# The last unit of a two-layer transformer kernel: full-row matmuls, token tile by token tile

## The chip, the cores and the metric

The kernel runs on one core of one Trainium2 chip. The metric is the device time of one execution in microseconds (us); the time before is the median of three runs. A profile is one further execution, with its own time. Its *span* runs from the first to the last instruction that the profiler recorded.

## What is computed

Two layers, each of attention and a feed-forward part, on x of 2048 tokens by 448 features, in float32:

```python
x = A_x
x = x + _A_ref(_layernorm(x, axis=-1), A_wq, A_wk, A_wv, A_wo)
x = x + _B_ref(_layernorm(x, axis=-1), B_w_gate, B_w_up, B_w_down)
x = x + _A_ref(_layernorm(x, axis=-1), A_wq, A_wk, A_wv, A_wo)
x = x + _B_ref(_layernorm(x, axis=-1), B_w_gate, B_w_up, B_w_down)
...
def _B_ref(x, w_gate, w_up, w_down):
    g = _silu(x @ w_gate)
    u = x @ w_up
    return (g * u) @ w_down
```

The attention (16 heads, one shared key and value head) is not touched by the change. The weights of the feed-forward part are 448 x 1792 (gate, up) and 1792 x 448 (down).

## The kernel before

**Products.** Every float32 operand is kept as a high part and a low part in TensorE's fp32r type. A product takes three passes: high by high, high by low, low by high. In names, `xh`/`xl` are the parts of the normalized x, `wgh`/`wgl` of the gate and up weights, `wdh`/`wdl` of the down weights, and `hh`/`hl` (both inside the tile `h`) of the hidden values g * u.

**Tiling of the feed-forward part.** Tokens come in 4 chunks `c` of 512 (4 token tiles `t` of 128 each), hidden features in 14 slices `fc` of 128, taken two at a time in 7 groups `fs`. For each group the kernel goes over the chunks, and for each chunk over the two slices. One such step is a *unit* (`unit`, L971): gate and up for 512 tokens and 128 hidden features into two PSUM banks `pg[0]` and `pg[1]`; then Silu on ScalarE (L1006), the product with up on VectorE (L1007), `hh` on ScalarE (L1008) and `hl` on VectorE (L1011). The *down* projection of the unit (`down`, L844) adds 4 token tiles of 128 x 448 into four banks `d[0]` to `d[3]`, which collect over the two slices of a group. After the second slice `accumulate` (L873) adds these banks to the residual `xres`: tiles 0, 1 and, in the last group of the last layer, 3 on VectorE (L881), tile 2 by a copy on ScalarE (L884) and an add on GpSimd (L885). In the last group of the last layer each tile is then stored to the output (L888) on SP's queue, except tile 2 of the last chunk, which goes on ScalarE's.

**Half rows.** 448 features are three blocks of 128 and one of 64. Most units split each matmul into two of 64 partitions that run side by side on the two halves of TensorE (`side_by_side`, L327; `by_rows`, L314): 11 pairs, then 10 pairs. Each half must write another bank than its neighbour, and the second set writes the bank that the first set's other half wrote. Between the sets `between` (L336) lets ScalarE copy one column out of each bank (tile `seen`, L339), so that the second set waits until the first is through. A down projection is done likewise: `step` runs 6 pairs (12 half-row matmuls), `between` touches the four banks, and a second `step` runs 6 pairs more. Only the first two units of each layer use full rows for gate and up (`product_T`, L304): 11 matmuls of 128 partitions per bank.

**Order of the work.** A unit does not run its own down projection. It leaves it in `self.pend`, a list of functions, and the next unit takes it: after the first 11 pairs it calls the first down step (L988), then it runs the 10 pairs; after Silu, the multiply and `hh` it calls the second down step, and behind that the adds of the chunk if there are any. What the last unit leaves is run by `flush` (L965): both steps of its down, then `add(0)`, then the other adds. The order of each engine's instructions is that of the program text. After `flush` each engine loads one value (`whole`) and branches past a second copy of the program, which these data never enter.

The *last unit* is layer 1, group 6, chunk 3, slice 13. The down ahead of it is that of slice 12, the one behind it that of slice 13; both write the same four banks, which the order rows below call bank4_17568, bank5_17569, bank6_78 and bank7_79 (tiles 0 to 3). Its gate and up write bank0_17564 and bank1_17565.

Of the kernel before, what the change touches and what calls it, by code (L numbers as in the profile page):

```python
# [15 lines left out]
P = 128  # L16
S = 2048
D = 448
# [5 lines left out]
NC = S // 512  # L24
NG = H // 4
NF = F // P
# [29 lines left out]
def forward(  # L56
# [14 lines left out]
    nc = tc.nc  # L71
# [39 lines left out]
    def bank(cands, hold=False):  # L111

        for _ in cands:
            turn[cands] = (turn.get(cands, -1) + 1) % len(cands)
            b = cands[turn[cands]]
            if b not in live:
                if hold:
                    live.add(b)
                return b, banks[b]
        raise AssertionError("no bank")  # L120

    def halves(name):

        return pers.tile([P, 2, 512], F32R, tag="halves", name=name, bufs=2)
# [151 lines left out]
    def natural(po, squares):  # L276

        if not squares:
            return po
        return po.rearrange("p (g t w) -> p t g w", g=4, w=32)  # L280

    def in_order(a, squares):

        return a.rearrange("p (t g w) -> p t g w", g=4, w=32) if squares else a
# [19 lines left out]
    def product_T(po, a_h, a_l, tiles):  # L304

        xh, xl = tiles[:2]
        seq = []
        for k in range(3):
            seq += [(a_h[k], xh[:, k, :]), (a_h[k], xl[:, k, :]), (a_l[k], xh[:, k, :])]
        seq += [(a_h[3], xh[:, 3, :]), (a_l[3], xh[:, 3, :])]  # L310
        for i, (a, b) in enumerate(seq):
            nc.tensor.matmul(po, a, b, start=(i == 0), stop=(i == len(seq) - 1))  # L312

    def by_rows(upper, n, w, tiles):  # L314

        h, l = w[:2]
        xh, xl, xd = tiles
        rs = slice(64, 128) if upper else slice(0, 64)
        seq = []
        for k in range(3):  # L320
            seq += [(h[rs, k, n, :], xh[rs, k, :]), (h[rs, k, n, :], xl[rs, k, :]), (l[rs, k, n, :], xh[rs, k, :])]
        seq.append((h[rs, 3, n, :], xh[rs, 3, :]))
        if n == upper:
            seq.append((l[rs, 3, n, :], xd[rs, :] if upper else xh[rs, 3, :]))
        return seq

    def side_by_side(lower, upper):  # L327

        assert len(lower) == len(upper)
        for two in zip(lower, upper):  # L330
            for po, (a, b), start, stop in two:
                nc.tensor.matmul(po, a, b, start=start, stop=stop, skip_group_check=True)  # L332
# [3 lines left out]
    def between(*pos):  # L336

        for i, po in enumerate(pos):
            nc.scalar.copy(seen[:, i : i + 1], po[:, 0:1])  # L339
# [495 lines left out]
    groups = [range(f, min(f + FG, NF)) for f in range(0, NF, FG)]  # L835

    class FeedForward:
# [6 lines left out]
        def down(self, fs, fc, d, hh, hl):  # L844


            _, _, dh, dl = self.W[fc]
            self.flip = 1 - self.flip
            one, two = ((0, 1), (2, 3)) if self.flip else ((2, 3), (0, 1))

            def step(ts, first):
                lists = []
                for upper, half in enumerate(ts):
                    rs = slice(64 * upper, 64 * upper + 64)
                    lists.append(
                        [
                            (
                                d[t][:, 0:D],
                                (a[rs, P * t : P * t + P], b[rs, :]),
                                first and fc == fs[0] and z == 0,  # L860
                                not first and fc == fs[-1] and z == 2,
                            )
                            for t in half
                            for z, (a, b) in enumerate(((hh, dh), (hh, dl), (hl, dh)))
                        ]
                    )
                side_by_side(*lists)
                if first:
                    between(*d)

            return [lambda: step((one, two), True), lambda: step((two, one), False)]

        def accumulate(self, gi, c, d):  # L873

            end = gi == len(groups) - 1
            last = end and self.layer == 1

            def add(t):
                r = xres[:, 4 * c + t, :]
                if t < 2 or (t == 3 and last):  # L880
                    nc.vector.tensor_tensor(r, d[t][:, 0:D], r, ALU.add)  # L881
                else:
                    s = self.stage.tile([P, 512], F32, name="stage")[:, 0:D]
                    nc.scalar.copy(s, d[t][:, 0:D])  # L884
                    nc.gpsimd.tensor_tensor(r, s, r, ALU.add)  # L885
                if last:
                    q = nc.scalar if t == 2 and c == NC - 1 else nc.sync
                    q.dma_start(outs[:, 4 * c + t, :], r)  # L888

            def others():  # L890
                for t in (1, 2, 3) if last else (2, 1, 3):
                    add(t)
                live.difference_update(HIGH)
                if end and self.nxt:
                    self.hand_over(c)

            return [lambda: add(0), others]
# [73 lines left out]
        def unit(self, gi, c, n):  # L971
            fs = groups[gi]
            fc = fs[n]
            w = self.W[fc]
            held, pg = zip(*(bank(LOW, True) for _ in range(2)))
            first, self.pend = self.pend, []
            if self.X[c][2] is not None:
                mid = self.mid.pop((gi, c, n), [])
                lists = [by_rows(upper, b, w, self.X[c]) for b in range(2) for upper in range(2)]
                ends = [(i == 0, False) for i in range(11)], [(False, i == 9) for i in range(10)]  # L980
                side_by_side(
                    [(pg[0], o, *e) for o, e in zip(lists[0], ends[0])],
                    [(pg[1], o, *e) for o, e in zip(lists[3], ends[0])],
                )
                between(*pg)
                for f in mid[:1]:
                    f()
                first.pop(0)()  # L988
                for f in mid[1:]:
                    f()  # L990
                side_by_side(
                    [(pg[1], o, *e) for o, e in zip(lists[2], ends[1])],
                    [(pg[0], o, *e) for o, e in zip(lists[1], ends[1])],
                )
            else:
                for b in range(2):
                    product_T(pg[b], *([v[:, k, b, :] for k in range(4)] for v in w[:2]), self.X[c])
                if first:
                    first.pop(0)()
                    self.left.append(first.pop(0))  # L1000
            live.difference_update(held)
            two = halves("h2")
            hh, hl = two[:, 0, :], two[:, 1, :]
            sg = pers.tile([P, 512], F32, name="sg")
            sq = c < NC - 1
            nc.scalar.activation(in_order(sg, sq), natural(pg[0], sq), AF.Silu)  # L1006
            nc.vector.tensor_tensor(in_order(sg, sq), natural(pg[1], sq), in_order(sg, sq), ALU.mult)  # L1007
            nc.scalar.copy(hh, sg)  # L1008
            for f in first[:2]:
                f()  # L1010
            nc.vector.tensor_tensor(hl, sg, hh, ALU.subtract)  # L1011
            for f in first[2:]:
                f()
            for e in list(self.soon):
                e[0] -= 1
                if e[0] < 0:
                    self.soon.remove(e)
                    e[1]()
            if n == 0:
                self.dn[c] = [bank(HIGH, True)[1] for _ in range(4)]  # L1020
            d = self.dn[c]
            self.pend = self.down(fs, fc, d, hh, hl)
            if n == len(fs) - 1:
                self.pend += self.accumulate(gi, c, d)
            if c == NC - 1 and fc + FG + 1 < NF:
                self.pend.append(lambda: self.W.__setitem__(fc + FG + 1, weights(fc + FG + 1)))
# [63 lines left out]
    fs, got = norm_steps(0)  # L1090
# [23 lines left out]
    for c in range(1, NC):  # L1114
        fs, got = norm_steps(c)
# [39 lines left out]
```

## Time and profile before

| | us |
|---|---|
| median of three runs | 1962.71 (1962.13 to 1963.45) |
| the profiled execution | 1962.25 |
| its span | 1960.4 |
| outside the span | 1.85 |
| mean granted TensorE clock | 0.998 of full |
| TensorE busy in the span | 1943.3 |
| start of the last unit, from the span's start | 1941.5 |

In the rows of the timeline the numbers are start and duration in us, then engine, line, operation, what is written from what is read, the partitions and columns, and how many instructions were merged into the row (x2). PE is TensorE's matmuls, PEld its weight loads, SPq and ACTq the queues from which SP and ScalarE issue DMAs. In the chain of waits a row is a piece of the chain that ended last. In a table of stretches the columns are the length, the busy time of PE, PEld, DVE, ACT and POOL, the granted clock, the DMA engines' share and GB/s.

### The profile page before, as it was taken

To read this page: it belongs to the slowest core of one execution; us is meant where nothing else is said; L and a number is where in the kernel's file an instruction comes from. 1 tells how busy PE (TensorE), PEld (TensorE's weight loads), DVE (VectorE), ACT (ScalarE), POOL (GpSimd) and SP (SyncE) were. 2 spreads that over 40 slices of the span, in tenths; PEclk is the share of its full clock that TensorE was granted. 3 is DMA by queue.
4 is the path that set the end of the run, shared out by engine and by line. 5 is a ranking of instruction groups with operands and counts; after the bars stand their busy time and mean duration, and the time that the engine had idled before them with its cause. 6 is when DMAs were issued, how large, how long until landed. Compare 5 with 4: busy or idle time off the path is not lost.

```text
span 1960.4 us, 44004 instructions
## 1 busy us (share of the span) xinstructions
PE 1943.3 (99%) x18469; PEld 1325.5 (68%) x18469; DVE 968.3 (49%) x1638; ACT 1264.1 (64%) x1888; POOL 553.6 (28%) x593
## 2 busy tenths in 40 slices
PE   9999999999999999999999999999999999999998
PEld 7544545445468999999974445454454799988886
DVE  6656575665743223223666565657656433223223
ACT  4899898998943333333349998989989333333332
POOL 4213123132214333333341221121231332323320
PEclk9999999999999999999999999999999999999999
DMA  5111011121130011110251110110211200011102
GB/s 166 55 36 29 21 40 40 29 53 43 26 87 20 17 32 32 32 29 19 67 156 34 37 30 22 50 28 24 67 40 32 71 28 21 17 32 32 32 2 77
DMA packets 100643, 83.61 MB, mean 43 GB/s; under 512 B 25080, under 2 KB 81656, under 8 KB 100440
## 3 DMA queue, kind: packets, MB, share of 16 engines
q1 hardware_dynamic: 98888, 79.55, 14.7%
q8 instruction: 145, 2.38, 0.5%
q10 hardware_dynamic: 1552, 1.20, 0.2%
q14 instruction: 58, 0.48, 0.1%
HBM read 57.38 MB, written 21.50 MB: 40 GB/s over the span
## 4 chain that ended last, share of the span: by engine, by line
PE 87%; ACT 9%; DMA 1%; DVE 1%; issue 1%; POOL 0%; SPq 0%; ACTq 0%; POOLq 0%; DVEq 0%
PE bank L332 40%; PE bank L688 20%; PE bank L633 14%; ACT pt L655 6%; PE three L633 5%; PE bank L312 4%; ACT pair L656 2%; PE three L612 2%; PE bank L612 1%; PE three L621 0%; PE bank L438 0%; DMA kt<-stage 0%; DMA xd<-xh 0%; DMA wr<-in_A_wq_dram 0%; DVE vt L546 0%
## 5 line engine op out<-in xcount | busy, mean ns | idle before, releaser
L655 ACT ACTIVATE pt<-three 128x1536 f32<-128x1536 f32 x512 | 723.0, 1484 | 52.9 <-PE three L633 52.9
L688 PE MATMUL bank<-pt,vsb 128*32 128x512 f32 x3072 | 490.8, 599 | 0.0
L688 PE MATMUL bank<-pair,vsb 128*32 128x512 f32 x1024 | 487.5, 598 | 0.6 <-ACT pair L656 0.6
L633 PE MATMUL bank<-qstack,keys 32*128 32x512 f32 x1536 | 473.1, 425 | 0.0
L332 PE MATMUL bank<-xh,wgh 64*128 64x512 f32 x1728 | 450.7, 389 | 0.0
L633 PE MATMUL three<-qstack,keys 32*128 32x512 f32 x4608 | 428.7, 408 | 0.5 <-ACT stage L539 0.3
L633 PEld LDWEIGHTS bank<-qstack,keys 32*128 32x128 f32 x1536 | 243.5, 183 | 250.0 <-issue 124.9
L654 DVE COPY pair<-bank 128x512 f32<-128x512 f32 x512 | 354.0, 691 | 95.2 <-PE bank L633 57.4
L332 PE MATMUL bank<-xh,wgl 64*128 64x512 f32 x1404 | 371.7, 391 | 0.0
L332 PE MATMUL bank<-xl,wgh 64*128 64x512 f32 x1296 | 338.1, 390 | 0.0
L332 PE MATMUL bank<-wdh,h 64*128 64x448 f32 x1792 | 334.3, 364 | 1.1 <-ACT h L1008 0.8
L1007 DVE TENSOR_TENSOR sg<-bank,sg 128x512 f32<-128x512 f32 x112 | 77.4, 691 | 502.5 <-ACT sg L1006 500.3
L656 ACT ACTIVATE pair<-pair 128x1024 f32<-128x1024 f32 x256 | 281.5, 1100 | 0.0
L332 PEld LDWEIGHTS bank<-xh,wgh 64*128 64x128 f32 x1728 | 266.3, 185 | 16.7 <-issue 1.3
L633 PEld LDWEIGHTS three<-qstack,keys 32*128 32x128 f32 x4608 | 261.5, 183 | 13.9 <-DVE xres L604 1.5
L885 POOL TENSOR_TENSOR xres<-stage,xres 128x448 f32<-128x448 f32 x108 | 127.3, 1197 | 502.5 <-ACT stage L884 502.3
L688 PEld LDWEIGHTS bank<-pt,vsb 128*32 128x32 f32 x3072 | 101.9, 109 | 246.0 <-issue 153.1
L332 PEld LDWEIGHTS bank<-wdh,h 64*128 64x128 f32 x1792 | 247.5, 184 | 14.8 <-issue 2.0
L697 DVE TENSOR_TENSOR o<-bank,o 128x512 f32<-128x512 f32 x224 | 154.9, 691 | 203.8 <-PE bank L688 203.8
L339 ACT COPY seen<-bank 128x1 f32<-128x1 f32 x664 | 81.9, 163 | 254.3 <-PE bank L332 251.2
L332 PEld LDWEIGHTS bank<-xh,wgl 64*128 64x128 f32 x1404 | 219.2, 184 | 13.8
L332 PE MATMUL bank<-wdl,h 64*128 64x448 f32 x896 | 222.2, 367 | 0.0
(145 smaller groups left out, 2095.7 us busy)
## 6 DMA issues: line engine op xcount, KB each, us to landing
o<-rd SPq DMA_DIRECT2D x32, 256.0 KB
qraw<-qd SPq DMA_DIRECT2D x128, 56.0 KB
qd<-stage SPq DMA_DIRECT2D x28, 224.0 KB
wdr<-in_B_w_down_dram SPq DMA_DIRECT2D x28, 224.0 KB
xt<-tb SPq DMA_DIRECT2D x24, 224.0 KB
wr<-in_B_w_gate_dram SPq DMA_DIRECT2D x28, 192.0 KB
wr<-in_B_w_up_dram SPq DMA_DIRECT2D x28, 192.0 KB
xn<-xt SPq DMA_DIRECT2D x6, 768.0 KB
```

The lines of the kernel that those rows point to most:

```text
L312: nc.tensor.matmul(po, a, b, start=(i == 0), stop=(i == len(seq) - 1))
L332: nc.tensor.matmul(po, a, b, start=start, stop=stop, skip_group_check=True)
L339: nc.scalar.copy(seen[:, i : i + 1], po[:, 0:1])
L612: nc.tensor.matmul(po[:, 0:D], a[:, g, P * t : P * t + P], b[:, g, :], start=False, stop=(g == NG - 1 and z == 2), skip_group_check=True,)
L633: nc.tensor.matmul(three[:, j, :] if j < 3 else one, k[js, kp, ks], q[js, part, :], start=(z == 0), stop=(z == 2), tile_position=(32 * j, 0),)
L654: copies.append(nc.vector.tensor_copy(pt1, one))
L655: es.append(nc.scalar.activation(pt, threes[y], AF.Exp, scale=SCALE))
L656: es.append(nc.scalar.activation(pair, pair, AF.Exp, scale=SCALE))
L688: nc.tensor.matmul(to[32 * j : 32 * j + 32, :], vsb[:, n % NT, :], pts[n][j], start=(y == 0), stop=(y == 1), skip_group_check=True,)
L697: f = nc.vector.tensor_tensor(accs[i][:, 0, :], to, accs[i][:, 0, :], ALU.add)
L885: nc.gpsimd.tensor_tensor(r, s, r, ALU.add)
L1007: nc.vector.tensor_tensor(in_order(sg, sq), natural(pg[1], sq), in_order(sg, sq), ALU.mult)
```

## The change

The last unit, and the downs of the last group of the last chunk, take another form:

- Gate and up of the last unit run in full rows with `product_T`: 11 matmuls for gate, then 11 for up, with no `between`.
- The down projections of slices 12 and 13 of chunk 3 run by a new function `by_tile`: for each token tile three full-row matmuls, 12 in all, no `between`. The down of slice 12 is called in one piece behind gate and up, where before half of it stood in the middle of them and half behind; a function that does nothing takes the place of its second step.
- The adds of the last chunk are all on VectorE, tile 2 too.
- The last chunk's tiles 1 and 3 are stored from ScalarE's queue, 0 and 2 from SP's (before: 2 from ScalarE's, the others from SP's).

```diff
@@ down @@
             _, _, dh, dl = self.W[fc]
+            if self.layer == 1 and d is self.dn.get(NC - 1) and fs is groups[-1]:
+                return [lambda: self.by_tile(fs, fc, d, ((hh, dh), (hh, dl), (hl, dh))), lambda: None]
             self.flip = 1 - self.flip
...
+        def by_tile(self, fs, fc, d, passes):
+
+            for t in range(4):
+                for z, (a, b) in enumerate(passes):
+                    nc.tensor.matmul(
+                        d[t][:, 0:D], a[:, P * t : P * t + P], b,
+                        start=(fc == fs[0] and z == 0), stop=(fc == fs[-1] and z == 2), skip_group_check=True,
+                    )
@@ accumulate @@
-                if t < 2 or (t == 3 and last):
+                if t < 2 or (last and (t == 3 or c == NC - 1)):
                     nc.vector.tensor_tensor(r, d[t][:, 0:D], r, ALU.add)
...
-                    q = nc.scalar if t == 2 and c == NC - 1 else nc.sync
+                    q = nc.scalar if t % 2 and c == NC - 1 else nc.sync
                     q.dma_start(outs[:, 4 * c + t, :], r)
@@ unit @@
-            if self.X[c][2] is not None:
+            if self.layer == 1 and c == NC - 1 and fc == NF - 1:
+                for b in range(2):
+                    product_T(pg[b], *([v[:, k, b, :] for k in range(4)] for v in w[:2]), self.X[c])
+                first.pop(0)()
+            elif self.X[c][2] is not None:
```

In the changed file the lines of `accumulate` and `unit` move down: L881 becomes L892, L888 L899, L1006 L1021, L1008 L1023; the matmuls of `by_tile` are L879.

How the change moves the instructions is seen at two places. First TensorE at the end of the program. Before, these twelve half-row matmuls, the second step of the last down, are the last it runs.

```order
L332 MATMUL bank4_17568<-wdh_21773,h2_22424 128x448
L332 MATMUL bank6_78<-wdh_21773,h2_22424 128x448
L332 MATMUL bank4_17568<-wdl_21774,h2_22424 128x448
L332 MATMUL bank6_78<-wdl_21774,h2_22424 128x448
L332 MATMUL bank4_17568<-wdh_21773,h2_22424 128x448
L332 MATMUL bank6_78<-wdh_21773,h2_22424 128x448
L332 MATMUL bank5_17569<-wdh_21773,h2_22424 128x448
L332 MATMUL bank7_79<-wdh_21773,h2_22424 128x448
L332 MATMUL bank5_17569<-wdl_21774,h2_22424 128x448
L332 MATMUL bank7_79<-wdl_21774,h2_22424 128x448
L332 MATMUL bank5_17569<-wdh_21773,h2_22424 128x448
L332 MATMUL bank7_79<-wdh_21773,h2_22424 128x448
```

The same engine at the same place after: the whole last down.

```order
L879 MATMUL bank4_17568<-wdh_21773,h2_22398 128x448
L879 MATMUL bank4_17568<-wdl_21774,h2_22398 128x448
L879 MATMUL bank4_17568<-wdh_21773,h2_22398 128x448
L879 MATMUL bank5_17569<-wdh_21773,h2_22398 128x448
L879 MATMUL bank5_17569<-wdl_21774,h2_22398 128x448
L879 MATMUL bank5_17569<-wdh_21773,h2_22398 128x448
L879 MATMUL bank6_78<-wdh_21773,h2_22398 128x448
L879 MATMUL bank6_78<-wdl_21774,h2_22398 128x448
L879 MATMUL bank6_78<-wdh_21773,h2_22398 128x448
L879 MATMUL bank7_79<-wdh_21773,h2_22398 128x448
L879 MATMUL bank7_79<-wdl_21774,h2_22398 128x448
L879 MATMUL bank7_79<-wdh_21773,h2_22398 128x448
```

The twelve rows of before are half of the down and go in pairs of two tiles; the twelve of after are all of it, and a tile is complete after each three.

Second ScalarE, from the hidden values of the unit ahead (h2_22336) to the end of the program, before (bank0 and bank1 are gate and up of the last unit, `seen` the copies of `between`).

```order
L339 COPY seen_107<-bank4_17568 128x1
L339 COPY seen_107<-bank5_17569 128x1
L339 COPY seen_107<-bank6_78 128x1
L339 COPY seen_107<-bank7_79 128x1
L1006 ACTIVATE sg_22425<-bank0_17564 128x512
L1008 CAST h2_22424<-sg_22425 128x512
L339 COPY seen_107<-bank4_17568 128x1
L339 COPY seen_107<-bank5_17569 128x1
L339 COPY seen_107<-bank6_78 128x1
L339 COPY seen_107<-bank7_79 128x1
L884 COPY stage_22474<-bank6_78 128x448
L888 DMA out_0_dram<-xres_89 128x448
```

And after, from the same point.

```order
L895 COPY stage_22358<-bank6_78 128x448
L1021 ACTIVATE sg_22399<-bank0_17564 128x512
L1023 CAST h2_22398<-sg_22399 128x512
L899 DMA out_0_dram<-xres_89 128x448 x2
L50 TENSOR_LOAD whole_61
L51 COMPARE_AND_BRANCH
```

All ten copies of `seen` of the last unit and of the last down are gone (two more stand just ahead of the rows of before), the copy of tile 2 too, and two stores stand at the end instead of one.

## The prediction

> **What bounds the kernel now.** I read the page first, then the chain of waits at its end, then the timeline of the last unit, then the stores.
>
> ```profile
> PE 1943.3 (99%) x18469; PEld 1325.5 (68%) x18469; DVE 968.3 (49%) x1638; ACT 1264.1 (64%) x1888; POOL 553.6 (28%) x593
> ```
>
> TensorE is busy for 99% of the span, so nothing can be won in the body by moving work between the other engines. The change touches only the last unit and what follows it, so the question is what the end costs. The chain of work that ended last, over the last 13 us (start, us, what):
>
> ```profile
> 1948.39 0.70 DVE sg L1007
> 1949.12 0.63 ACT h L1008
> 1949.76 0.70 DVE h L1011
> ...
> 1951.70 0.23 ACT seen L339 x2
> ...
> 1953.37 0.62 DVE xres L881
> 1954.00 0.69 POOL xres L885
> ```
>
> Until 1947.7 the chain is TensorE alone. From there it runs through Silu, multiply, hh and hl, then through the small copies of L339, then the residual adds. The timeline of the same stretch shows what that does to TensorE (x2 is a side-by-side pair; the number in brackets is idle time and its releaser):
>
> ```profile
> 1941.29 0.36 PE L332 MATMUL bank<-wdh,h 64*128 64x448 f32 x2
> ...
> 1947.32 0.40 PE L332 MATMUL bank<-xh,wgh 64*128 64x512 f32 x2
> 1947.56 0.37 PE L332 MATMUL bank<-wdh,h 64*128 64x448 f32 x2
> ...
> 1948.58 0.36 PE L332 MATMUL bank<-wdh,h 64*128 64x448 f32 x2
> 1949.79 0.47 PE L332 MATMUL bank<-wdh,h 64*128 64x448 f32 x2 [0.84 <-ACT h L1008]
> ...
> 1950.51 0.68 PE L332 MATMUL bank<-wdh,h 64*128 64x448 f32 x4
> ...
> 1951.97 0.47 PE L332 MATMUL bank<-wdh,h 64*128 64x448 f32 x1 [0.17 <-ACT seen L339]
> ...
> 1952.28 0.77 PE L332 MATMUL bank<-wdh,h 64*128 64x448 f32 x4
> ...
> 1952.76 1.77 DVE L881 TENSOR_TENSOR xres<-bank,xres 128x448 f32<-128x448 f32 x3 [2.30 <-PE bank L332]
> 1952.89 0.57 PE L332 MATMUL bank<-wdh,h 64*128 64x448 f32 x2
> ...
> 1953.55 1.14 POOL L885 TENSOR_TENSOR xres<-stage,xres 128x448 f32<-128x448 f32 x1 [9.36 <-ACT stage L884]
> ```
>
> The unit's first gate/up pair follows the row at 1941.29, and its last starts at 1947.32. Six pairs of the previous down then cover the handover until 1948.8, but h arrives at 1949.79: a hole of 1.0 us. Inside the last down TensorE waits again, for hl (1950.51) and for the L339 copies (1951.97). Its last matmul ends at 1952.89 + 0.57 = 1953.46, VectorE's three adds end at 1952.76 + 1.77 = 1954.53, GpSimd's at 1954.69. The rest up to 1960.4 is stores and closing, below.
>
> **The change, part by part.** The full-row form stands elsewhere in this trace: the first two units (L312) and the output projection (L612). The first number of a row is its start:
>
> ```profile
> 1529.96 0.39 PE L312 MATMUL bank<-xh,wgl 128*128 128x512 f32 x1
> 1530.19 0.39 PE L312 MATMUL bank<-xh,wgh 128*128 128x512 f32 x1
> 1530.39 0.60 ACT L1006 ACTIVATE sg<-bank 128x512 f32<-128x512 f32 x1 [0.58 <-PE bank L312]
> ...
> 1532.45 0.39 PE L312 MATMUL bank<-xh,wgl 128*128 128x512 f32 x1
> 1532.95 0.69 DVE L1007 TENSOR_TENSOR sg<-bank,sg 128x512 f32<-128x512 f32 x1 [1.07 <-PE bank L312]
> ...
> 1537.44 0.39 PE L312 MATMUL bank<-xh,wgl 128*128 128x512 f32 x1
> ...
> 1547.86 0.37 PE L332 MATMUL bank<-wdh,h 64*128 64x448 f32 x2
> 1548.16 0.47 PE L612 MATMUL bank<-woh,onh 128*128 128x448 f32 x1
> 1548.47 0.36 PE L612 MATMUL bank<-wol,onh 128*128 128x448 f32 x1
> ...
> 1550.49 0.37 PE L612 MATMUL bank<-woh,onl 128*128 128x448 f32 x1
> ```
>
> From 1530.19 to 1537.44 there are 32 steps: 0.227 us for a full-row matmul of 512 columns. From 1548.47 to 1550.49 there are 10: 0.202 us for 448. Going from half rows to full rows takes 0.30 and 0.31 for the first two steps, so the switch costs 0.2 once. Half-row pairs step by about 0.23 and 0.205, so a full-row matmul costs what a pair costs.
>
> TensorE then. Last half-row pair at 1941.29; first gate matmul 0.30 later, 1941.59; the second 1941.90; the 22nd 20 x 0.227 later, 1946.43. The first down starts at 1946.66 and its 12 matmuls at 0.202 leave the last down to start at 1949.08. That one's twelfth starts at 1951.30 and ends 0.37 later, at 1951.67, **1.8 us before** 1953.46, if nothing waits. Of this, about 2.1 are waits that go (1.0 for h, the rest hl, the L339 copies, and pairs fallen out of step); some 0.3 come on, from the switch and from one matmul more (22 against 21 pairs), with slightly shorter steps.
>
> Does anything wait? Silu starts 0.43 after gate's last matmul (1529.96 to 1530.39), so at 1944.4, under the up matmuls: free. The multiply starts 0.50 after up's last (1532.45 to 1532.95): 1946.93. hh starts 0.73 later (1948.39 to 1949.12), 1947.66, and releases TensorE 0.67 after that (1949.12 to 1949.79), 1948.33: 0.75 before the last down wants it. hl starts 0.64 after hh and releases 0.75 after that (1949.76 to 1950.51): 1949.05, 0.44 before the third matmul of the last down (1949.49). The first down's 2.4 us are the cover; without it the handover would show as 2.1 us. VectorE's multiply now waits for TensorE itself; behind it are only hl and the four adds.
>
> Adds: before, tile 0's last matmul started at 1952.28 and its add at 1952.76, 0.48 later. After, tile 0's third matmul starts at 1949.49, its add at 1949.97, and four adds of 0.62 end at 1952.44; tile 3's own matmul (1951.30 + 0.48 + 0.62) gives 1952.40. So the last data stands at about 1952.44, **2.1 us before** 1954.53. ScalarE's copy and GpSimd's add of tile 2 vanish; they ended beside VectorE's adds, so this is worth 0.1 at most, and VectorE's fourth add is in the sum.
>
> The one shape not in this trace is h as stationary operand in full rows. Bounds: 0.202 a matmul (L612, same columns), or that plus a whole load of 0.188 (row under the rivals), 24 x 0.188 = 4.5 us more; nothing below, since pairs and full rows stream alike. I take 0.202, the nearest row.
>
> Stores: the issues (start, us), and the DMA's share of time and GB/s in stretches (last two columns).
>
> ```profile
> 1942.35 0.33 SPq L888 DMA_DIRECT2D out_dram<-xres  x1
> ...
> 1944.64 0.41 SPq L888 DMA_DIRECT2D out_dram<-xres  x1
> ...
> 1954.03 1.31 SPq L888 DMA_DIRECT2D out_dram<-xres  x1
> ...
> 1955.43 0.90 SPq L888 DMA_DIRECT2D out_dram<-xres  x1
> ...
> 1943.20:1943.90 0.70, 0.70 (x10) 0.58 (x8) 0.70 (x2) 0.00 (x0) 0.70 (x1) 1.00 0.82 315
> 1943.90:1944.50 0.60, 0.60 (x10) 0.52 (x8) 0.33 (x1) 0.23 (x2) 0.29 (x1) 1.00 0.00 0
> ...
> 1945.40:1946.50 1.10, 1.10 (x14) 0.88 (x12) 0.00 (x0) 0.29 (x3) 0.00 (x0) 1.00 0.87 329
> 1946.50:1947.50 1.00, 1.00 (x12) 0.84 (x10) 0.00 (x0) 0.00 (x0) 0.00 (x0) 1.00 0.03 8
> ...
> 1957.50:1958.15 0.65, 0.00 (x0) 0.00 (x0) 0.00 (x0) 0.00 (x0) 0.00 (x0) 0.50 0.20 68
> 1958.15:1958.60 0.45, 0.00 (x0) 0.00 (x0) 0.00 (x0) 0.00 (x0) 0.00 (x0) 0.50 0.00 0
> ```
>
> In the chunk before, an issue takes 0.33 to 0.41, and its traffic is over 1.55 us after the issue for a store alone (1942.35 to 1943.90) and about 1.9 for the fourth in a row (1944.64 to 1946.5). At the end, tile 1's issue holds SP's queue for 1.31, so tile 3, ready at 1954.53, is issued at 1955.43, takes 0.90, and its traffic ends at 1958.1, 2.7 after the issue. From there to the end of the span are 2.3 us of closing (1958.1 to 1960.4) that no edit touches.
>
> After, tile 3 goes out on ScalarE's queue, which has held nothing since hh but tile 1's store, 0.04 after its add: 1952.48. Its traffic lasts 1.55 to 2.7; I take 1.9, the store in a quick row, as these are 0.62 apart. That gives 1954.4, and with 2.3 of closing an end at **1956.7, 3.7 us earlier**.
>
> The 3.7 splits so: 1.8 TensorE, 0.3 adds, 0.85 the late issue, 0.8 the slow landing. The Trainium skill, "DMA: Bandwidth & Descriptors", section "Issuing engines are not separate DMA queues", says that DMAs from different engines run on the same 16 DMA engines, and that issuing from several saves only the sequencer's time. By that rule the second queue would earn at most the 0.85, and the 0.8 would stay; the profiled end, with a store on ScalarE's queue among three on SP's and traffic still crawling at 68 GB/s, does not contradict it.
>
> **Rivals.**
> 1. *The stores stay slow.* If the 1.31 and 0.90 come from the DMA engines and not from SP's queue, ScalarE's issue stalls alike: 0.85 and 0.8 stay. Gain 1.8 + 0.3 = 2.1, time 1960.6. For: the issue of tile 3 was slow although tile 1's was over. Against: four stores in the chunk before, closer together, all took under 0.42.
> 2. *The stores run clear.* Traffic over 1.55 after the issue, as for the store alone: 1952.48 + 1.55 + 2.3 = 1956.3, gain 4.1, time 1958.6. For: spacing 0.62 against some 0.55 of traffic each. Against: so far the end was never clear.
> 3. *Slower: weight loads come into the open.* A half-row load can run beside the other half's matmul; a full-row load has no such half.
>
> ```profile
> L612 PEld LDWEIGHTS bank<-woh,onh x24: 186/188/189, 572.4 to 1549.9; 128*128 128x128 f32 x24
> ```
>
> Each takes 0.188. Were it in the open for all 46 full-row matmuls, 8.6 us come on, less 3.7: 4.9 slower, 1967.6. It decides from 3.7/46 = 0.08 a matmul on. Against: the same rows step by 0.202 with that load hidden. The Trainium skill, "TensorE: Matmul & The Clock Gate", section "Step-by-step: what each phase is for", lets a load be pulled ahead if row groups don't conflict or if it goes to the background buffer; only the second is left for full rows. The L612 steps say that the second suffices.
> 4. *The handover still shows.* If hl comes more than 0.44 later than worked out, the excess is lost; 1 us of it would leave 2.7, time 1960.0. Nothing speaks for it.
>
> That the change misses its unit is excluded: the rows of the order show both downs of the last group in the new form.
>
> **How the numbers follow.** The profiled execution took 1962.25, its span 1960.4 and 1.85 around it. It lies 0.46 under the median, 1962.71, and within the three runs (1962.13 to 1963.45). The sum gives 1958.55 by that execution; I lay the 3.7 on the median: **1959.0**. Chances: forecast 0.60 (1958.6 to 1959.8, its landing between 1.55 and 2.7), rival 1 0.20, rival 2 0.14, rival 3 0.03, rival 4 0.03. The range takes both store rivals in, with 0.2 to 0.4 on either side for the spread of runs: 1958.2 to 1960.8. A measurement of this kernel can tell about 0.2% from no change, here 3.9 us, so below 1958.8 is faster: rival 2 and some three tenths of the forecast, 0.32. Slower over 0.2% is rival 3: 0.03. Same: 0.65.
>
> **What would show it.** Right: the gate rows of the last unit at 0.227 and L879 rows at 0.202 with no idle in brackets; the last L879 matmul at about 10.0 us after the unit's first; four adds in one row on VectorE, ending some 0.8 us after TensorE; the last ScalarE issue 0.04 after the last add and taking under 0.5; traffic over 1.9 later. Wrong: an idle mark at the last down (rival 4), steps of 0.3 or more (rival 3), a ScalarE issue of about 1 us or traffic over 2.5 us after it (rival 1), or an end that comes more than 2.4 us after the last traffic, a closing that I took as fixed.

## The result and the profile after

| | before | after |
|---|---|---|
| median of 21 runs, us | 1962.71 (1961.14 to 1964.36) | 1959.26 (1957.95 to 1959.87) |
| ratio | | 0.9982, 95% interval 0.9976 to 0.9988 |
| profiled execution, us | 1962.25 | 1958.55 |
| its span, us | 1960.4 | 1956.8 |

The kernel is 3.45 us faster by the medians, 3.6 by the spans of the two profiles. That is 0.18%: a ratio of 1 lies outside the interval, but the gain stays below the 0.2% from which the prediction would have called it faster. The forecast was 1959.0, range 1958.2 to 1960.8.

The page after still shows TensorE busy for 99%, now of a shorter span:

```profile
span 1956.8 us, 43898 instructions
PE 1942.8 (99%) x18425; PEld 1328.7 (68%) x18425; DVE 969.6 (50%) x1639; ACT 1262.7 (65%) x1877; POOL 553.9 (28%) x592
```

The timeline of the last unit after:

```profile
1940.44 0.60 ACT L1021 ACTIVATE sg<-bank 128x512 f32<-128x512 f32 x1 [1.96 <-PE bank L332]
...
1941.26 0.37 PE L332 MATMUL bank<-wdh,h 64*128 64x448 f32 x2
1941.56 0.49 PE L312 MATMUL bank<-xh,wgh 128*128 128x512 f32 x1
...
1941.89 0.39 PE L312 MATMUL bank<-xl,wgh 128*128 128x512 f32 x1
...
1944.40 0.60 ACT L1021 ACTIVATE sg<-bank 128x512 f32<-128x512 f32 x1 [1.55 <-PE bank L312]
...
1946.47 0.40 PE L312 MATMUL bank<-xh,wgl 128*128 128x512 f32 x1
1946.70 0.37 PE L879 MATMUL bank<-wdh,h 128*128 128x448 f32 x1
...
1946.97 0.69 DVE L1022 TENSOR_TENSOR sg<-bank,sg 128x512 f32<-128x512 f32 x1 [2.77 <-PE bank L312]
...
1947.70 0.62 ACT L1023 CAST h<-sg 128x512 fp32r<-128x512 f32 x1 [2.70 <-DVE sg L1022]
...
1948.35 0.69 DVE L1026 TENSOR_TENSOR h<-sg,h 128x512 fp32r<-128x512 f32 x1 [0.69 <-ACT h L1023]
...
1949.98 2.54 DVE L892 TENSOR_TENSOR xres<-bank,xres 128x448 f32<-128x448 f32 x4 [0.94 <-PE bank L879]
...
1951.43 0.37 PE L879 MATMUL bank<-wdh,h 128*128 128x448 f32 x1
```

No PE row has an idle mark any more: gate, up and both downs run from 1941.56 to 1951.80 without a stop. Silu, multiply, hh and hl lie under them, and the adds follow the tiles, ending at 1949.98 + 2.54 = 1952.52.

The four store issues after, and the stretches of DMA traffic (last two columns: share and GB/s):

```profile
1950.63 0.33 SPq L899 DMA_DIRECT2D out_dram<-xres  x1
1951.26 0.37 ACTq L899 DMA_DIRECT2D out_dram<-xres  x1
1951.94 0.49 SPq L899 DMA_DIRECT2D out_dram<-xres  x1
1952.56 0.36 ACTq L899 DMA_DIRECT2D out_dram<-xres  x1
...
1953.60:1954.40 0.80, 0.00 (x0) 0.00 (x0) 0.00 (x0) 0.00 (x0) 0.00 (x0) 1.00 0.73 275
1954.40:1954.70 0.30, 0.00 (x0) 0.00 (x0) 0.00 (x0) 0.00 (x0) 0.00 (x0) 1.00 0.11 45
1954.70:1955.20 0.50, 0.00 (x0) 0.00 (x0) 0.00 (x0) 0.00 (x0) 0.00 (x0) 1.00 0.05 16
```

No issue takes over 0.5, against 1.31 and 0.90 before. But a thin remainder of store traffic still runs until 1954.7.

The body ahead of the last unit drifts by a microsecond or so from one execution to the next, so ends are best compared from a common point. I call **tail** the time from the start of the Silu ahead of the last unit (1940.44 in the first row above, 1940.46 before) to the end of the span. All times in the tables below count from there; "traffic" is the end of the last data packet of the stores in the trace. One profile (kernel before, late branch) had a lower mean granted clock, 0.874, and so a span of 2075.7, but its TensorE and VectorE rows in the tail agree with those of before to 0.01 us, only its tail is used, and the medians in the table of runs leave such executions out.

| from the Silu | before | after | gain of this step |
|---|---|---|---|
| last matmul ends | 13.00 | 11.35 | 1.65 |
| last add on VectorE ends | 14.06 | 12.09 | 0.32 more |
| last store issued | 14.96 | 12.12 | 0.87 more |
| traffic ends | 17.64 | 14.24 | 0.56 more |
| span ends (the tail) | 19.95 | 16.38 | 0.17 more, 3.57 in all |

### The profile page after: what moved, and what is told of

Same layout as the page of the kernel before. It is cut to its first block, busy times and chain, and to the rows that moved or that the text cites. A ratio compares the mean times of both kernels' runs of the same rounds, so it can differ in the third digit from the quotient of the medians.

```text
span 1956.8 us, 43898 instructions
## 1 busy us (share of the span) xinstructions
PE 1942.8 (99%) x18425; PEld 1328.7 (68%) x18425; DVE 969.6 (50%) x1639; ACT 1262.7 (65%) x1877; POOL 553.9 (28%) x592
## 3 DMA queue, kind: packets, MB, share of 16 engines
q10 hardware_dynamic: 1696, 1.43, 0.2%
## 5 line engine op out<-in xcount | busy, mean ns | idle before, releaser
L332 PE MATMUL bank<-wdh,h 64*128 64x448 f32 x1760 | 328.3, 363 | 0.0
L339 ACT COPY seen<-bank 128x1 f32<-128x1 f32 x654 | 80.7, 163 | 250.4 <-PE bank L332 247.5
```

## The experiments

Two theories stood against each other on the stores. **T** is the prediction's: the slow issues came from crowding on SP's queue, which the second queue relieves. **C** came up on reading the DMA packets: a load of program code holds up a part of one store, and what stands behind that store on the same queue waits too. In TensorE's program the branch past the second copy follows the last matmuls, and 1.1 us after TensorE's sequencer takes it a load of 16 KB starts. The DMA view by queue kind shows it between the stores' own traffic (packets, MB, share), first in the kernel before, from 1953.3 to 1954.9:

```profile
q1 hardware_dynamic: 131, 0.22, 35.0%
q8 instruction: 1, 0.02, 4.7%
```

and in the changed kernel, from 1950.3 to 1952.0:

```profile
q1 hardware_dynamic: 109, 0.20, 29.5%
q8 instruction: 1, 0.02, 4.3%
```

That one packet lasts from 13.31 to 14.50 of the tail before, and from 10.45 to 11.62 after. Tile 0's store is in flight then in both. By 14.5 (before) all but eight of its 128 packets of 1792 bytes are through, and those eight run singly until 15.4: as many as one of 16 DMA engines carries.

All runs, with medians against the kernel before on the same chip:

| run | last matmul | last add (VectorE) | last issue | traffic | tail | against before | medians, us | ratio (95%) |
|---|---|---|---|---|---|---|---|---|
| before | 13.00 | 14.06 | 14.96 | 17.64 | 19.95 | | | |
| after | 11.35 | 12.09 | 12.12 | 14.24 | 16.38 | -3.57 | -3.45 | 0.9982 (0.9976 to 0.9988) |
| last down only | 12.36 | 13.09 | 13.12 | 16.18 | 18.44 | -1.51 | -1.43 | 0.9990 (0.9981 to 0.9999) |
| handover only | 12.12 | 13.39 | 13.86 | 16.93 | 19.21 | -0.74 | -0.85 | 0.9994 (0.9985 to 1.0003) |
| queues only | 13.00 | 14.06 | 15.79 | 17.99 | 20.24 | +0.29 | +0.35 | 1.0000 (0.9991 to 1.0009) |
| adds and queues | 13.00 | 14.60 | 14.63 | 16.99 | 19.20 | -0.75 | -0.84 | 0.9995 (0.9986 to 1.0004) |
| after, GpSimd add | 11.35 | 12.09 | 13.04 | 14.84 | 17.08 | -2.87 | -2.74 | 0.9985 (0.9976 to 0.9994) |
| after, old queues | 11.35 | 12.09 | 12.36 | 15.01 | 17.36 | -2.59 | -2.21 | 0.9989 (0.9980 to 0.9998) |
| after, one queue | 11.35 | 12.09 | 12.39 | 14.94 | 17.27 | -2.68 | -2.01 | 0.9990 (0.9981 to 0.9999) |
| before, no branch | 13.00 | 14.06 | 14.26 | 16.28 | 17.82 | -2.13 | -1.73 | 0.9989 (0.9980 to 0.9998) |
| after, no branch | 11.35 | 12.08 | 12.12 | 13.72 | 15.60 | -4.35 | -4.20 | 0.9981 (0.9972 to 0.9990) |
| before, late branch | 13.00 | 14.06 | 14.25 | 17.26 | 19.65 | -0.30 | -0.35 | 0.9999 (0.9990 to 1.0008) |
| after, late branch | 11.35 | 12.09 | 12.12 | 13.73 | 15.84 | -4.11 | -4.21 | 0.9979 (0.9969 to 0.9988) |
| after, late branch, one queue | 11.35 | 12.09 | 12.12 | 13.68 | 15.79 | -4.16 | -4.06 | 0.9980 (0.9971 to 0.9989) |

The late-branch rows leave the added transpose out of "last matmul".

The intervals of the ratios are about 0.0009 to each side, 1.8 us. So no median here tells one variant of the changed kernel from another, and gains of less than 1 us over the kernel before are not clear of noise either. The steps below are read from the traces, one for each run. In these the columns of TensorE and VectorE repeat to 0.01 us wherever an edit leaves them alone. The columns of the stores also carry the length of the code load, which was 0.96 to 1.65 us, and how far they repeat was not measured.

### TensorE: the last down only, and the handover only

```diff
 last down only (the changed kernel's condition, narrowed; gate, up and the down ahead
 in half rows; queues as before; adds all on VectorE)
-            if self.layer == 1 and d is self.dn.get(NC - 1) and fs is groups[-1]:
+            if self.layer == 1 and d is self.dn.get(NC - 1) and fc == NF - 1:
...
 handover only (last down in half rows; adds and queues as before)
+            if self.layer == 1 and d is self.dn.get(NC - 1) and fc == NF - 2:
```

> The kernel before with only the last down projection (slice 13) tile by tile in full rows, and the adds of the last chunk all on VectorE; gate, up and the down ahead as before, queues as before. T: the hole for h stays (1.0 us), the waits inside the last down go but that for hl; its last matmul ends 0.7 us earlier (about 1952.7), the last add 1.1 us earlier, the time falls by 1.1 us, and by up to 0.9 more if the late issue goes as well. Rival (the waits inside the last down are only that for hl, the rest is drift between pairs that costs nothing): last matmul less than 0.3 us earlier.

> The kernel before with only the handover: gate and up of the last unit in full rows, the down of slice 12 in full rows behind them, the last down in half rows with its copies of L339, adds and queues as before. T: h and hl are there in time, the last down starts about 0.7 us earlier (1949.1) and its last matmul ends 0.6 to 0.9 us earlier, after a second switch (0.2) back to half rows; the time falls by 0.6 to 0.9 us. Rival (the hole moves into the last down): the wait at the copies of L339 grows, the last matmul is at most 0.2 us earlier.

With the last down only, TensorE's rows keep both waits of the handover, and lose all others:

```profile
1949.05 0.37 PE L332 MATMUL bank<-wdh,h 64*128 64x448 f32 x2
1950.25 0.47 PE L879 MATMUL bank<-wdh,h 128*128 128x448 f32 x1 [0.84 <-ACT h L1019]
1950.56 0.36 PE L879 MATMUL bank<-wdl,h 128*128 128x448 f32 x1
1950.98 0.68 PE L879 MATMUL bank<-wdh,h 128*128 128x448 f32 x2
```

The step of 0.42 ahead of the last row is the wait for hl. The last matmul ends 0.64 earlier and the last add 0.97 earlier, close to the 0.7 and 1.1 expected; the issue is no longer late (13.12, 0.03 behind the add), so it comes 1.84 earlier than before. But the landing got longer, 3.06 after the issue instead of 2.68, and the tail gained 1.51.

With the handover only, the last down starts on time and then waits for the copies of L339:

```profile
1950.54 0.47 PE L332 MATMUL bank<-wdh,h 64*128 64x448 f32 x2
...
1951.67 0.37 PE L332 MATMUL bank<-wdh,h 64*128 64x448 f32 x2
1952.35 0.47 PE L332 MATMUL bank<-wdh,h 64*128 64x448 f32 x2 [0.31 <-ACT seen L339]
```

From 1951.67 to 1952.35 are 0.68, where a step is 0.205: the wait at the copies is there as before (an idle mark of 0.31, before 0.17), but the rival, that it eats the gain, fails: the last matmul ends 0.88 earlier, the tail is 0.74 shorter. The two parts together, 1.51 + 0.74 = 2.25, come near to the change with the old queues, 2.59; where the other 0.34 comes from is not shown.

### Adds and queues

```diff
 queues only: the kernel before, and adds and queues: both edits
-                    q = nc.scalar if t == 2 and c == NC - 1 else nc.sync
+                    q = nc.scalar if t % 2 and c == NC - 1 else nc.sync
...
-                if t < 2 or (t == 3 and last):
+                if t < 2 or (last and (t == 3 or c == NC - 1)):
...
 after, GpSimd add: the changed kernel with the first line of the second pair back
```

> The kernel before with one edit: tiles 1 and 3 of the last chunk are stored from ScalarE's queue, 0 and 2 from SP's. Theory T (as predicted: the issue of 1.31 us and the late, slow store of tile 3 come from crowding on SP's queue): tile 3 is issued at about 1954.6 in under 0.45 us, traffic ends near 1956.5, the time falls by up to 1.6 us. Rival C (TensorE's code load after its branch, 16 KB from 1953.77 to 1954.97 on one DMA engine, holds up the parts of every store that run on that engine; a queue then only decides who waits behind whom): one of the four issues is still over 0.8 us, traffic ends at 1957.2 or later, the time falls by 0.5 to 1.0 us.

> The kernel before with two edits together: all adds of the last chunk on VectorE, and tiles 1 and 3 stored from ScalarE's queue. The queues alone lengthened the tail by 0.3 us because ScalarE's store of tile 1 stood ahead of its copy of tile 2. If that is the whole reason, GpSimd is out of it now: VectorE's fourth add ends at about 14.7 (0.6 later than before), no issue is over 0.85 us, traffic ends 2.1 to 2.7 us after the last issue at 14.7, 16.8 to 17.4, the tail is 0.2 to 0.8 us shorter than before. If two queues do nothing on the half-row end, the tail is not shorter than before.

> The changed kernel with the add of tile 2 in the last chunk as before (ScalarE's copy 0.53, GpSimd's add 1.14). T: tile 2's sum is there only at about 1951.24 + 0.06 + 0.53 + 0.07 + 1.14 = 1953.0, 0.5 us after tile 3's, its store becomes the last, and the time is 0.4 to 0.6 us longer than the changed kernel's. Rival (as the prediction priced this edit by itself, 0.1 at most): the store of tile 2 hides behind that of tile 3, no more than 0.1 us is lost.

Both theories missed the queues alone: the tail grew by 0.29. The timeline says why:

```profile
1954.75 0.37 ACTq L888 DMA_DIRECT2D out_dram<-xres  x1
1955.22 0.53 ACT L884 COPY stage<-bank 128x448 f32<-128x448 f32 x1 [2.51 <-DVE xres L881]
...
1955.83 1.13 POOL L885 TENSOR_TENSOR xres<-stage,xres 128x448 f32<-128x448 f32 x1 [10.90 <-ACT stage L884]
```

In ScalarE's program the store of tile 1, which waits for VectorE's add, stands ahead of the copy of tile 2. So the copy starts at 14.03 of the tail, where before it started at 12.48, GpSimd's add ends at 15.77 of the tail instead of 14.23, and tile 2 becomes the last store. With the adds on VectorE as well that path is gone, and the tail is 0.75 shorter than before, at the upper end of what was expected. The two edits belong together.

The same holds from the other side. In the changed kernel with GpSimd's add, the copy waits behind ScalarE's store of tile 1 again: it starts at 11.27, 0.41 later than the expectation had it. GpSimd ends at 13.02, 0.93 after VectorE's last add, and 0.70 of the gain is lost. The expectation had 0.4 to 0.6, without the wait behind the store.

### The second queue

```diff
 after, old queues
+                    q = nc.scalar if t == 2 and c == NC - 1 else nc.sync
...
 after, one queue
+                    q = nc.sync
```

> The changed kernel with the stores as before: tile 2 from ScalarE's queue, 0, 1 and 3 from SP's. T: tile 1 holds SP's queue for about 1.3 us, tile 3 is issued late and lands slowly, the time is 1.5 us longer than the changed kernel's (some 2.1 under the kernel before). C: tile 1's issue is slow behind tile 0's held-up part, but the code load lies earlier against the last store (1950.9 to 1952.1), so tile 3 is issued within 0.4 us of its add and the time is 0 to 0.5 us longer than the changed kernel's.

> The changed kernel with all four stores of the last chunk on SP's queue. T: at least the 1.5 us of the two queues are lost. C: tile 1's issue is slow (about 1 us), tiles 2 and 3 follow in row, tile 3 is issued 0.3 to 0.9 us late: 0.3 to 0.8 us longer than the changed kernel. If issuing costs nothing but its own 0.33 us, nothing is lost, as adds come 0.62 us apart.

In the tail both lose about 0.9 of the 3.57 (0.98 and 0.89), between what T and C had given; the medians put it at 1.24 and 1.44, within their noise. The issues on SP's queue are, first with the old queues, then with one queue (x4: shortest, median, longest in ns):

```profile
L899 SPq DMA_DIRECT2D out_dram<-xres x3: 332/417/1459, 1951.6 to 1953.8; - x3
```

```profile
L899 SPq DMA_DIRECT2D out_dram<-xres x4: 333/396/1007, 1950.9 to 1953.1; - x4
```

Tile 1's took 1.46 with the old queues and 1.0 with one. Tile 3 went out only 0.24 and 0.27 later than in the changed kernel; the rest came in the landing, 2.65 and 2.55 after the issue against 2.12. So the second queue earns, but these runs do not tell T from C.

### Without the branch, and with a late one

```diff
 no branch (from the kernel before, and from the changed one)
-    ok = nc.values_load(whole[0:1, 0:1].bitcast(mybir.dt.int32), ...
-    with tc.If(ok == 0, label="again"):
-        forward(tc, None, True, *aps)
...
-                        tc.mark_branch_hint_location("again", engines=(...))
...
 late branch (from the kernel before, and from the changed one)
             self.flush()
+            if self.layer == 1 and fine is not None:
+                nc.tensor.transpose(bank(LOW)[1][:, 0:P], xres[:, NT - 1, 0:P], ident)
```

> The kernel before without the load of the checked value, the branch and the second copy of the program, so without the repeat that a failed check would start (the test is left out). T: the stores crowd as before, tile 1's issue over 1 us, tile 3's issue 0.9 us late; only the engines' loads and branches at the end go. C: no code load falls into the stores, all four issues take under 0.45 us, tile 3 is issued at once after its add and its traffic is over 1.6 to 1.9 us later, 1.5 us earlier than before against the last add.

> The changed kernel without the load of the checked value, the branch and the second copy of the program (the test and the repeat are left out). T: 3.6 us under the kernel before without them. C: only what TensorE and VectorE gain is left between the two, 2.0 to 2.3 us, since the late issue and the slow landing went in both; traffic is over 1.55 to 1.9 us after the last issue, not 2.1.

> The kernel before with one small transpose on TensorE that waits for the last add, so TensorE's branch and its 16 KB code load come some 2.5 us later; nothing else is moved. Times are from the start of the Silu ahead of the last unit. C (that one load made tile 1's issue slow): tile 1's issue takes 0.33 to 0.45 us instead of 1.31, tile 3 is issued at about 14.1 instead of 15.0, traffic ends at 16.3 to 17.2 (other engines' loads of 8 KB still fall into it) instead of 17.64, the tail is 0.5 to 1.4 us shorter. T (crowding on SP's queue): tile 1's issue stays over 1 us and the tail is as long as before.

> The changed kernel with the same transpose. C: the 16 KB load moves from 10.45 to about 13.8, behind most of the stores; all four issues take under 0.4 us, traffic ends at 13.7 to 13.9 instead of 14.24 (without any branch: 13.72), the tail is 0.3 to 0.5 us shorter, below what the time of a run can tell. T: no change.

> The changed kernel with the transpose and with all four stores on SP's queue. C (two queues earn only because tile 0's part behind TensorE's code load blocks what stands behind it on the same queue): with the load out of the way one queue is as good, all issues under 0.45 us, traffic ends within 0.2 us of that of the changed kernel with the transpose. T (one queue is crowded by itself): the 0.9 us that one queue cost the changed kernel are lost here too.

The kernel before without a branch has the same three stores on SP's queue and the same times of the adds, and every issue on that queue takes 0.33:

```profile
L885 SPq DMA_DIRECT2D out_dram<-xres x3: 332/332/333, 1954.9 to 1956.0; - x3
```

Between the two kernels without a branch only 2.22 are left (17.82 against 15.60), as C had it. T, which had 3.6, falls. C's expectation for the traffic of the kernel before was missed by a little: it ends 2.22 after VectorE's last add, 1.36 sooner than with the branch, where 1.5 had been expected.

The late branch narrows it to TensorE's own load: the added transpose reads the last tile, so TensorE cannot reach its branch before the last add; nobody reads what it writes. In the kernel before it moves that load from 13.31 to 16.20 and leaves the rows of TensorE and VectorE where they were; the issues shrink from 1.31 and 0.90 to 0.33:

```profile
L888 SPq DMA_DIRECT2D out_dram<-xres x3: 332/332/333, 2069.0 to 2070.2; - x3
```

The tail gained only 0.30, less than C's 0.5 to 1.4: the load now falls into the traffic of the last store (16.20 to 17.30), which ends at 17.26, and loads of 8 KB on another instruction queue at 15.2 to 15.8 fall among the stores too. In the changed kernel the late load (14.60 to 15.58) misses the traffic, which ends at 13.73, as without any branch (13.72), and the tail is 0.54 shorter still. And there one queue is as good as two (15.79 against 15.84), where it had cost 0.89 with the load in the way:

```profile
L899 SPq DMA_DIRECT2D out_dram<-xres x4: 332/332/333, 1951.2 to 1953.1; - x4
```

The changed kernel with the late branch, with either choice of queues, has the shortest tail of all that keep the test and the repeat. Its ratio to the kernel before, 0.9979, does not stand apart from the change's own 0.9982.

The traces hold one more sign for C, in the seven runs where both kinds of issue start during the load: one as the first of the last chunk on ScalarE's queue, one behind another store on its queue. The first takes 0.37 in each; the second takes 0.50 to 1.46, also on ScalarE's queue (queues only, 0.84). With the last down only, tile 1's issue on SP's queue starts 0.09 ahead of the load and takes 0.33.

## Why the prediction was right, step by step

The forecast held: 1959.0 against 1959.26, 3.7 against 3.57 in the tail. Its steps:

- **TensorE, 1.8 forecast, 1.65 measured.** The switch took 0.30 and 0.33 (forecast 0.30 and 0.31), gate and up step by (1946.47 - 1941.89) / 20 = 0.229 (0.227), the downs by (1951.43 - 1946.70) / 23 = 0.206 (0.202). The last difference, over 23 steps, is 0.09 of the 0.15 that the gain fell short by. h as a stationary operand in full rows cost what the nearest row said, with its load hidden: rival 3 fell.
- **The handover under the first down.** Silu at 1944.40 (forecast 1944.4), multiply 1946.97 (1946.93), hh 1947.70 (1947.66), hl 1948.35 (1948.30). No wait was left, so rival 4 fell. The cover is shown by the run with the last down only, where both waits are back.
- **The adds, 0.3 forecast, 0.32 measured.** They ended at 1952.52, forecast 1952.44.
- **The late issue, 0.85 forecast, 0.87 measured**, and **the slow landing, 0.8 forecast, 0.56 measured**: traffic lasted 2.12 after the issue, not 1.9. The sizes were about right, the cause was not. The prediction put both on SP's queue. For the late issue the runs show TensorE's code load in the way of a store: without it three or four stores on SP's queue each go out in 0.33. Rival 1, that the DMA engines themselves were slow, had the better half of the cause, but not its result: in the changed kernel the last store stands on a queue with no held-up store ahead, and goes out 0.03 after its add.
- **What makes the landing slow is shown in part.** Without a branch the traffic ends 2.02 (before) and 1.60 (after) behind the last issue. With TensorE's load late it is 1.61 in the changed kernel, so that load cost 0.51 of its 2.12. In the kernel before it is 3.01, as the load then falls into the last store, and the loads of 8 KB stay; no run moves those alone. The 1.9 of the forecast came from a place in the trace with no code load among the stores (there the packets themselves end 1.78 after the issue), so that it lay near 2.12 was luck, and the closing, 0.16 shorter than forecast, made up for most of the miss.
- **The closing of 2.3, "that no edit touches"**, was 2.14. That it depends on the branch is shown by the runs without one, 1.54 (before) and 1.88 (after).
- **GpSimd's add "worth 0.1 at most"** was priced in the order of before. In the order of after it is worth 0.70, also because the copy stands behind a store on ScalarE and starts 0.41 late. This was in the sum all the same, as the forecast had counted the four adds on VectorE only.

The Trainium skill, "DMA: Bandwidth & Descriptors", section "Issuing engines are not separate DMA queues", has it that a second issuing engine saves only sequencer time. The late-branch runs agree: 15.79 with one queue, 15.84 with two. The runs with the code load do not: 0.89 for the second queue, of which the issue is 0.27. The same page of the Trainium skill, section "Queues, rings and completion order", gives every queue a ring of its own on every DMA engine, and lets an engine take turns among its rings. With that, what stands behind a stuck store on one ring waits, and what stands on another does not. This fits the eight late packets, but which DMA engine carried which packet is not in the trace, so that part is argued, not shown.

## What to carry to other kernels

At the end of a kernel price the whole path from the last matmul to the last landed store, with rows from a place in the same trace where the form already stands; here every step came out within 0.25 us, two of them for another reason than forecast. Before a second queue is given the credit for a quick store, look for what else the DMA engines move then, code loads behind a branch above all, and look at what a store that waits holds up in its issuing engine's program.

## What was not expected of the hardware

- TensorE's sequencer reaches the branch 2 us before its last matmul ends (9.30 against 11.35 in the changed kernel; 12.17 against 13.00 before), and the load of code starts 1.15 later, in the middle of the kernel's last stores. Over the runs with the branch it starts 1.14 to 1.24 later, in one 1.61. It takes 0.96 to 1.65 us for 16 KB in these runs.
- A store's issue that starts while such a load runs, behind a store on the same queue, took 0.50 to 1.46 us instead of 0.33.
- One engine's branch, delayed by a transpose that nobody reads, shortened the tail of the changed kernel by 0.54 us.
